# One core, three layers in one kernel: where low parts are made, in which order a mixture unit issues its steps, and when chunk loads go out

## The chip, the cores and the metric

The kernel runs on one core of one Trainium2 chip. The metric is the device time of one execution in microseconds; lower is better. The core's engines are TensorE (PE in the rows, PEld its weight loads), VectorE (DVE), ScalarE (ACT), GpSimd (POOL) and SyncE (SP), which issues most of the DMAs. Each engine works through its own queue in order.

## What is computed

The reference chains three layers. A Nyström attention over 4 batches, 8 heads and 576 positions gives a table of 2304 tokens by 512. Then a dense layer with a softplus in the middle, and then a layer of eight experts, of which each token uses one:

```python
h = x @ w_in                                        # 2304x512 by 512x2048
g = np.maximum(h, 0.0) + np.log1p(np.exp(-np.abs(h)))
x = g @ w_out                                       # 2304x2048 by 2048x512
logits = x @ w_gate;  e_idx = np.argmax(logits, 1)  # one of 8 experts per token
eom = 1 / (1 + np.exp(-(x @ w_output_gate)))
for e in range(8):
    h = np.maximum(x[mask] @ w1[e], 0.0)
    out[mask] = gate_w[mask, None] * eom[mask, e, None] * (h @ w2[e])
```

The weights of the dense layer arrive as 64-bit floats.

## The kernel before

**Products.** Every fp32 operand of the dense layer and the experts is kept as a high part (`hi`, an ACT copy to a shorter format) and a low part (`lo`, the rest: value minus high part, a subtraction on DVE or POOL). A product is three matmuls: hi by hi, hi by lo, lo by hi.

**The dense layer** (called mixture here) runs over nine chunks of 256 tokens and, in each, over eight pieces p of two 128-wide columns of `w_in`. One chunk and one piece make a unit, and the list `order` has 72 of them, i = 0 to 71. A unit issues: `gemm1`, 24 matmuls of 256 columns into `ps_h`; `softplus`, which makes `gh` and `gl`; and `gemm2`, 12 matmuls of 512 columns into the accumulators of its chunk, which is issued two units later (`LAG` = 2). So PE alternates between `gemm1(i)` and `gemm2(i-2)`. `ps_h` has two buffers, so `gemm1(i+2)` needs that `d` of unit i (the last pass that reads `ps_h`) is over.

**softplus** is four ACT passes (`t` by Abs, `t` by Exp, `u`, `l` by Ln), three DVE passes (`u`, `d`, `l`), the ACT pass `gh` (the high part of l) and the DVE pass `gl`. In the kernel before, all of it is issued in one go, ahead of `gemm2(i-2)`.

**Joint units.** The first 24 units (`nj` = 24, i = 0 to 23) go through chunks 0, 1 and 2 together, piece by piece, because the weights are still being decoded from 64-bit words then: piece p+1 of chunk 0, then piece p of chunks 1 and 2. The decode is 21 jobs, one for each 128-wide slice f of `w_in` (`whi`, `wlo`) or of `w_out` (`woh`, `wol`) that the attention stage has not prepared, in the order in which they are due. A job has three steps, taken with `units(n)`: `hi` (ACT, and the Abs of the next job, `deca`), `lo` (DVE), and the next job's three DVE passes (`dect`, `dect`, `deca`) with a load. `units(1)` stands at three places of softplus, so each unit from i = 1 does the work of one job; `EXTRA = 0, 5, 8` adds one more job in units 5 and 8.

**Chunks.** From unit 24 on, each chunk has eight units of its own. In its unit p = 5 it loads the next chunk (`load_xr`, SP) and splits it at once (`split_x`: `xh` on ACT, `xl` on DVE). Chunk 3 (`JOINT`) is loaded and split in unit 23. When `gemm2` has finished a chunk, its `gate` begins: two ACT copies of the accumulators (`x`, L679), transposes (`ps_tr` on PE, copied to `x2t` on ACT), logits (`ps_lg`), the choice of the expert and the rank (`sb`, `cd`, `oh`, `ps_rk`, `rmat`). `gate` is a generator in steps; one step is taken after `gemm1` (`next(side)`) and one after `gemm2`. In the units in which chunk 7 is gated (`fast`), further steps stand in the middle of `gemm1` and `gemm2` (`hook`). `early` follows the gate of chunk 7 (`ps_n`, `erhs`, `ps_i`) and finds the tokens of the first two expert slots.

**Expert slots.** A slot is 128 tokens of one expert. `splits` gives, eight steps a slot, the halves u = 0, 1 of four weight blocks i = 0 to 3: `hi` on ACT (L477), `lo` on DVE or POOL (L479). In slot 0 the four halves of blocks 2 and 3 and the second half of block 0 go to POOL. The gate of the last chunk and `route`, which assigns all other slots, run on DVE inside slots 0 and 1; the registers that choose the later weights come out of `route`.

The order of all queues from the mixture on is the program's own order (`manual_schedule`).

Of the kernel before, what the change touches and what calls it, by code (L numbers as in the profile page):

```python
# [12 lines left out]
F32R = DT.float32r  # L13
# [17 lines left out]
CH = 256  # L31
# [85 lines left out]
def moe_nystrom_kernel(ctx: ExitStack, tc: tile.TileContext, q, k, v, w_in, w_out, w_gate, w_ogate, w1, w2,  # L117
# [357 lines left out]
    def split(s, i, w, u):  # L475
        us = slice(2 * u, 2 * u + 2)
        nc.scalar.activation(w[0][:, us], raw[i][:, us], AF.Copy)  # L477
        eng = nc.gpsimd if s == 0 and i > 1 or i % 2 == 0 and u else nc.vector
        eng.tensor_tensor(w[1][:, us], raw[i][:, us], w[0][:, us].bitcast(F32), ALU.subtract)  # L479
# [65 lines left out]
    with ExitStack() as mctx:  # L545
# [94 lines left out]

        def softplus(h, units):

            t = sp.tile([128, 2, CH], F32, tag="t", name="t")
            u = sp.tile([128, 2, CH], F32, tag="u", name="u")
            l = sp.tile([128, 2, CH], F32, tag="l", name="l")
            d = sp.tile([128, 2, CH], F32, tag="d", name="d")
            gh = m3.tile([128, 2, CH], F32R, tag="gh", name="gh")
            gl = m3.tile([128, 2, CH], F32R, tag="gl", name="gl")
            nc.scalar.activation(t, h, AF.Abs)
            nc.scalar.activation(t, t, AF.Exp, scale=-1.0)  # L650
            nc.scalar.activation(u, t, AF.Identity, bias=1.0)  # L651
            nc.scalar.activation(l, t, AF.Ln, bias=1.0)
            units(1)
            nc.vector.scalar_tensor_tensor(u, u, -1.0, t, ALU.add, ALU.subtract)  # L654
            nc.vector.scalar_tensor_tensor(d, h, 0.0, u, ALU.max, ALU.subtract)  # L655
            nc.vector.tensor_tensor(l, l, d, ALU.add)  # L656
            nc.scalar.activation(gh, l, AF.Copy)  # L657
            units(1)
            nc.vector.tensor_tensor(gl, l, gh.bitcast(F32), ALU.subtract)  # L659
            units(1)  # L660
            return gh, gl

# [190 lines left out]
        with tc.manual_schedule():  # L853
# [28 lines left out]
            for i in range(len(order) + LAG):  # L882
# [11 lines left out]
                if i < len(order):  # L894
                    c, p = order[i]
                    if i == nj - 1:
                        xr.append(load_xr(JOINT))
                    h = gemm1(p, xs[c], *HB.get(i, ()))
                    if i > nj + LAG:
                        next(side, None)  # L900
                    gs[i] = softplus(h, units if i else int)
                    if i in EXTRA:
                        units(1 if i == 0 else 3)
                    if i == 2:
                        nc.vector.tensor_copy(tri_b, cc("tri"))
                        nc.vector.tensor_copy(one_b, cc("ones"))
                        nc.vector.memset(osum[:, 0], 0.0)
                        nc.vector.tensor_copy(sgn[:, 0], cc("iota")[:1, :NE])
                        nc.vector.tensor_scalar(sgn[:, 1], cc("iota")[:1, :NE], -1.0, None, ALU.mult)
                        for nm, src in ((0, w_gate), (1, w_ogate)):  # L910
                            nc.sync.dma_start(wg[:, :, nm * NE:(nm + 1) * NE], src.rearrange("(k p) e -> p k e", p=128))
# [178 lines left out]
```

## Time and profile before

| | |
|---|---|
| time, median of 3 runs | 910.09 us (909.3 to 910.9) |
| profiled execution | 910.2 us, of which the span from first to last instruction is 908.4 us |
| busy: PE, PEld | 859.9 us (95%), 718.9 us (79%) |
| busy: DVE, ACT, POOL | 666.5 us (73%), 586.9 us (65%), 209.5 us (23%) |
| mean granted TensorE clock | 0.988 of full speed |
| attention stage, joint units | to about 152 us; to 284 us |
| chunks 3 to 8 (units 24 to 71) | 284 to 600 us |
| expert slots | 600 to 908 us |

PE's busy share is modelled from its issue times, so what is read is its idle time: where PE waits, for whom, and how long the matmuls behind the wait take. A wait is put down to the releaser that came last. Times below are microseconds from the start of the span.

### The profile page before, as it was taken

Reading aid. Unit: us, or ns where it says so; the run is one execution under the profiler, and the core shown is the slowest. Engines: PE = TensorE matmul, PEld = TensorE weight load, DVE = VectorE, ACT = ScalarE, POOL = GpSimd, SP = SyncE. Lnnn points to the kernel's source line nnn. Section 1 sums busy time; section 2 is a strip of 40 time slices with the busy share of each in tenths; the row PEclk is TensorE's granted clock in tenths of the full one; section 3 lists DMA queues with packets and bytes.
Section 4 is the critical chain, followed back from the end, with each engine's and each line's share of the span. In section 5 each row is a group of like instructions: output and inputs, shape, how many; then the busy total and the mean of one; then the engine's idle time right before and its main releaser. Section 6 shows DMA issues by size and latency. Waiting matters only on the chain.

```text
span 908.4 us, 15419 instructions
## 1 busy us (share of the span) xinstructions
PE 859.9 (95%) x5826; PEld 718.9 (79%) x5826; DVE 666.5 (73%) x1121; ACT 586.9 (65%) x958; POOL 209.5 (23%) x109
## 2 busy tenths in 40 slices
PE   6998987989998999998999998989999999999996
PEld 3665655888997999998899997877888888888885
DVE  0856697999984465556556463668799999999994
ACT  2554565767774655555455554465888888888883
POOL 0001131000000000000000000034666667666662
PEclk9999999999999999999999999999999999999998
DMA  9856555333300000101011000141118369521600
GB/s 222 196 140 183 158 189 166 95 116 97 113 24 24 1 25 1 47 24 47 1 48 47 1 25 1 47 186 59 36 40 292 148 222 366 185 105 35 232 26 33
DMA packets 49516, 90.92 MB, mean 100 GB/s; under 512 B 5471, under 2 KB 32095, under 8 KB 47392
## 3 DMA queue, kind: packets, MB, share of 16 engines
q1 hardware_dynamic: 41408, 74.43, 26.6%
q0 software_dynamic: 3680, 10.78, 3.7%
q10 hardware_dynamic: 4352, 4.72, 1.5%
q8 instruction: 46, 0.75, 0.4%
q14 instruction: 30, 0.25, 0.1%
HBM read 134.46 MB, written 15.48 MB: 165 GB/s over the span
## 4 chain that ended last, share of the span: by engine, by line
PE 68%; DVE 14%; DMA 6%; ACT 6%; issue 4%; POOL 0%; SPq 0%; DVEq 0%; POOLq 0%; ACTq 0%
PE ps_h L635 19%; PE acc L670 15%; PE ps_g L960 10%; PE ps_y L985 9%; DMA raw<-in_moe_w 3%; DVE lo L479 2%; DVE dect L101 2%; PE ps_hT L974 2%; ACT hi L477 2%; PE ps_lg L695 2%; DVE deca L102 1%; PE ps_t L185 1%; PE ps_t L161 1%; DVE l L656 1%; DVE d L655 1%
## 5 line engine op out<-in xcount | busy, mean ns | idle before, releaser
L479 DVE TENSOR_TENSOR lo<-raw,hi 128x1024 fp32r<-128x1024 f32 x129 | 226.3, 1781 | 11.4 <-ACT hi L477 11.1
L477 ACT ACTIVATE hi<-raw 128x1024 fp32r<-128x1024 f32 x176 | 176.9, 1063 | 8.5 <-DMA raw<-in_moe_w 8.1
L635 PE MATMUL ps_h<-xh,whi 128*128 128x256 f32 x512 | 148.1, 289 | 7.7 <-DVE d L655 4.8
L635 PE MATMUL ps_h<-xl,whi 128*128 128x256 f32 x512 | 146.3, 286 | 0.4 <-DVE xl L108 0.4
L635 PE MATMUL ps_h<-xh,wlo 128*128 128x256 f32 x512 | 146.2, 286 | 0.0
L486 POOL DMA_INDIRECT xg<-x_d,gidx x23 | 37.0, 1610 | 444.1 <-ACT t L650 433.1
L479 POOL TENSOR_TENSOR lo<-raw,hi 128x1024 fp32r<-128x1024 f32 x47 | 116.7, 2485 | 35.8 <-ACT hi L477 35.6
L657 ACT ACTIVATE gh<-l 128x512 fp32r<-128x512 f32 x72 | 45.5, 632 | 116.0 <-DVE l L656 116.0
L654 DVE SCALAR_TENSOR_TENSOR u<-u,t 128x512 f32<-128x512 f32 x72 | 49.6, 688 | 83.5 <-ACT u L651 83.4
L635 PEld LDWEIGHTS ps_h<-xh,whi 128*128 128x128 f32 x512 | 99.2, 194 | 13.6 <-DVE d L655 6.1
L670 PE MATMUL acc<-woh,gh 128*128 128x512 f32 x256 | 103.1, 403 | 1.6 <-ACT gh L657 1.6
L670 PE MATMUL acc<-wol,gh 128*128 128x512 f32 x256 | 101.0, 394 | 0.0
L635 PEld LDWEIGHTS ps_h<-xl,whi 128*128 128x128 f32 x512 | 99.2, 194 | 2.2 <-DVE xl L108 0.6
L670 PE MATMUL acc<-woh,gl 128*128 128x512 f32 x256 | 100.8, 394 | 0.0
L635 PEld LDWEIGHTS ps_h<-xh,wlo 128*128 128x128 f32 x512 | 99.4, 194 | 0.0
L659 DVE TENSOR_TENSOR gl<-l,gh 128x512 fp32r<-128x512 f32 x72 | 49.9, 693 | 38.8 <-ACT gh L657 37.0
L985 PE MATMUL ps_y<-hi,woh 128*128 128x512 f32 x184 | 76.7, 417 | 0.2 <-ACT woh L977 0.2
L985 PE MATMUL ps_y<-hi,wol 128*128 128x512 f32 x184 | 73.3, 398 | 1.4 <-DVE wol L978 1.3
L960 PE MATMUL ps_g<-hi,x0l 128*128 128x512 f32 x184 | 73.9, 402 | 0.3
L985 PE MATMUL ps_y<-lo,woh 128*128 128x512 f32 x184 | 72.7, 395 | 0.0
L960 PE MATMUL ps_g<-hi,x0h 128*128 128x512 f32 x184 | 72.1, 392 | 0.0
L960 PE MATMUL ps_g<-lo,x0h 128*128 128x512 f32 x184 | 71.9, 391 | 0.0
(246 smaller groups left out, 1756.6 us busy)
## 6 DMA issues: line engine op xcount, KB each, us to landing
raw<-in_moe_w SPq DMA_DIRECT2D x88, 1024.0 KB
raw<-in_moe_w_in SPq DMA_DIRECT2D x16, 512.0 KB
raw<-in_moe_w_out SPq DMA_DIRECT2D x16, 512.0 KB
x_d<-x SPq DMA_DIRECT2D x9, 514.0 KB
k<-in_k SPq DMA_DIRECT2D x8, 576.0 KB
q<-in_q SPq DMA_DIRECT2D x8, 576.0 KB
v<-in_v SPq DMA_DIRECT2D x8, 576.0 KB
xT_d<-xo ACTq DMA_DIRECT2D x16, 288.0 KB
```

The source lines that it names most:

```text
L101: nc.vector.scalar_tensor_tensor(t, hi32, -0x80000000, t, ALU.bitwise_and, ALU.bitwise_or)
L477: nc.scalar.activation(w[0][:, us], raw[i][:, us], AF.Copy)
L479: eng.tensor_tensor(w[1][:, us], raw[i][:, us], w[0][:, us].bitcast(F32), ALU.subtract)
L486: nc.gpsimd.indirect_dma_start(out=xg, out_offset=None, in_=src, in_offset=bass.IndirectOffsetOnAxis(ap=gidx[:, s:s + 1], axis=0))
L635: nc.tensor.matmul(ps[:, i], a[:, kk], b_[:, kk], start=n == 0, stop=n == 11)
L654: nc.vector.scalar_tensor_tensor(u, u, -1.0, t, ALU.add, ALU.subtract)
L657: nc.scalar.activation(gh, l, AF.Copy)
L659: nc.vector.tensor_tensor(gl, l, gh.bitcast(F32), ALU.subtract)
L670: nc.tensor.matmul(acc[tt], a[:, i, ts_], b_[f], start=f == 0 and n == 0, stop=f == NFF - 1 and n == 2)
L695: nc.tensor.matmul(pl[:, :2 * NE], xt[tt][:, kk], wg[:, kk], start=kk == 0, stop=kk == 3)
L960: nc.tensor.matmul(ps, a[:, kk], b_[:, kk], start=n == 0, stop=n == 11)
L985: nc.tensor.matmul(y, a[:, kk], b_[:, kk], start=half == 0 and n == 0, stop=half == 1 and n == 11)
```

## The change

Six edits. `EXTRA` becomes three further steps in unit 15 instead of those in units 5 and 8. The weight steps are taken only in joint units. `softplus` becomes a generator in four parts: `gemm1(i)`, the gate step behind it and the four ACT passes come first, then the three DVE passes, then `gemm2(i-2)`, the first ACT copies of a gate, and the gate step behind `gemm2`, and only then `gh`, a weight step, `gl`. `load_xr` moves from p = 5 to the end of p = 3 (chunk 3: unit 21), `split_x` stays at p = 5 (chunk 3: unit 22 instead of 23). And all eight low parts of slot 0 go to DVE.

```diff
-EXTRA = 0, 5, 8
+EXTRA = 15, 15, 15
...
-        eng = nc.gpsimd if s == 0 and i > 1 or i % 2 == 0 and u else nc.vector
+        eng = nc.gpsimd if s and i % 2 == 0 and u else nc.vector
...
             nc.scalar.activation(l, t, AF.Ln, bias=1.0)
-            units(1)
+            yield
             nc.vector.scalar_tensor_tensor(u, u, -1.0, t, ALU.add, ALU.subtract)
             nc.vector.scalar_tensor_tensor(d, h, 0.0, u, ALU.max, ALU.subtract)
             nc.vector.tensor_tensor(l, l, d, ALU.add)
+            yield
+            gh = m3.tile([128, 2, CH], F32R, tag="gh", name="gh")
+            gl = m3.tile([128, 2, CH], F32R, tag="gl", name="gl")
             nc.scalar.activation(gh, l, AF.Copy)
-            units(1)
+            yield
             nc.vector.tensor_tensor(gl, l, gh.bitcast(F32), ALU.subtract)
-            units(1)
-            return gh, gl
+            yield gh, gl
...
                     c, p = order[i]
-                    if i == nj - 1:
-                        xr.append(load_xr(JOINT))
-                    h = gemm1(p, xs[c], *HB.get(i, ()))
+                    g = softplus(gemm1(p, xs[c], *HB.get(i, ())))
                     if i > nj + LAG:
                         next(side, None)
-                    gs[i] = softplus(h, units if i else int)
-                    if i in EXTRA:
-                        units(1 if i == 0 else 3)
...
-                    if i == nj - 1:
-                        xs[JOINT] = split_x(xr.pop(0))
-                    if p == 5 and JOINT - 1 < c < NCH - 1:
-                        xs[c + 1] = split_x(load_xr(c + 1))
+                    next(g)
+                    if 0 < i < nj:
+                        units(1)
+                    next(g)
...
                 if nj + LAG < i < len(order) + LAG - 1:
                     next(side, None)
+                if i < len(order):
+                    next(g)
+                    if 0 < i < nj:
+                        units(1)
+                    gs[i] = next(g)
+                    if i < nj:
+                        units(1 + EXTRA.count(i))
...
+                    if i == nj - 3 or p == 3 and JOINT - 1 < c < NCH - 1:
+                        xr.append(load_xr(max(c + 1, JOINT)))
+                    if i == nj - 2 or p == 5 and JOINT - 1 < c < NCH - 1:
+                        xs[max(c + 1, JOINT)] = split_x(xr.pop(0))
```

PE's queue holds the same instructions in the same order in both kernels. Three places of the other queues follow.

DVE in unit 15 and the beginning of the next. The rows of one job are `wlo` or `wol` (its low part; 2002 is the tile of slices 8 to 15 of `w_in`) and `dect`, `dect`, `deca` (the decode of the next one). Before:

```order
L654 SCALAR_TENSOR_TENSOR u<-u,t 128x512
L655 SCALAR_TENSOR_TENSOR d<-ps_h,u 128x512
L656 TENSOR_TENSOR l<-l,d 128x512
L599 TENSOR_TENSOR wol_2071<-deca,woh_2058 128x512
L659 TENSOR_TENSOR gl<-l,gh 128x512
L100 TENSOR_SCALAR dect<-deca 128x512
L101 SCALAR_TENSOR_TENSOR dect<-raw,dect 128x512
L102 SCALAR_TENSOR_TENSOR deca<-raw,dect 128x512
```

Now:

```order
L652 SCALAR_TENSOR_TENSOR u<-u,t 128x512
L653 SCALAR_TENSOR_TENSOR d<-ps_h,u 128x512
L654 TENSOR_TENSOR l<-l,d 128x512
L599 TENSOR_TENSOR wlo_2002<-deca,whi_2001 128x4x128
L660 TENSOR_TENSOR gl<-l,gh 128x512
L100 TENSOR_SCALAR dect<-deca 128x512
L101 SCALAR_TENSOR_TENSOR dect<-raw,dect 128x512
L102 SCALAR_TENSOR_TENSOR deca<-raw,dect 128x512
L599 TENSOR_TENSOR wol_2070<-deca,woh_2057 128x512
L100 TENSOR_SCALAR dect<-deca 128x512
L101 SCALAR_TENSOR_TENSOR dect<-raw,dect 128x512
L102 SCALAR_TENSOR_TENSOR deca<-raw,dect 128x512
```

The decode stands two jobs further back than before: unit 15 now makes the low part of slice 13 of `w_in` (before, unit 13 did), and unit 18 that of slice 15. Slice 13 is read by `gemm1` of unit 16, in its second half, and slice 15 by that of unit 19; on PE these matmuls carry a wait for DVE.

ACT in units 65 and 66, where the gate of chunk 7 begins (6256 and 6252 are the same tile in the two kernels). Before:

```order
L652 ACTIVATE l<-t 128x512
L657 ACTIVATE gh<-l 128x512
L679 ACTIVATE x_6256<-acc_5816 128x512
L679 ACTIVATE x_6256<-acc_5817 128x512
L690 ACTIVATE x2t<-ps_tr 128x512
L649 ACTIVATE t<-ps_h 128x512
L650 ACTIVATE t<-t 128x512
L651 ACTIVATE u<-t 128x512
L652 ACTIVATE l<-t 128x512
L657 ACTIVATE gh<-l 128x512
L690 ACTIVATE x2t<-ps_tr 128x512
```

Now:

```order
L650 ACTIVATE l<-t 128x512
L679 ACTIVATE x_6252<-acc_5812 128x512
L679 ACTIVATE x_6252<-acc_5813 128x512
L658 ACTIVATE gh<-l 128x512
L690 ACTIVATE x2t<-ps_tr 128x512
L647 ACTIVATE t<-ps_h 128x512
L648 ACTIVATE t<-t 128x512
L649 ACTIVATE u<-t 128x512
L650 ACTIVATE l<-t 128x512
L690 ACTIVATE x2t<-ps_tr 128x512
L658 ACTIVATE gh<-l 128x512
```

The accumulator copies and the second `x2t` have changed places with `gh`.

DVE in slot 0, from the rank of the last chunk to `rmat`. Before:

```order
L732 TENSOR_TENSOR z<-lg,oh 128x16
L733 TENSOR_REDUCE s_6882<-z 128x2
L736 TENSOR_TENSOR cd<-ps_rk,oh 128x16
L737 TENSOR_REDUCE rk<-cd 128x2
L740 TENSOR_TENSOR q__6890<-rk,cst 128x34
L742 TENSOR_REDUCE rd<-q__6890 128x2
L743 SCALAR_TENSOR_TENSOR rk<-rd,rk 128x2
L978 TENSOR_TENSOR wol_79<-ps_hT,woh_76 128x512
L978 TENSOR_TENSOR wol_80<-ps_hT,woh_77 128x512
L746 TENSOR_SCALAR rmat<-cst,rk 128x128 x2
```

Now:

```order
L479 TENSOR_TENSOR lo_6803<-raw_6701,hi_6802 128x1024 x2
L732 TENSOR_TENSOR z<-lg,oh 128x16
L733 TENSOR_REDUCE s_6882<-z 128x2
L736 TENSOR_TENSOR cd<-ps_rk,oh 128x16
L737 TENSOR_REDUCE rk<-cd 128x2
L740 TENSOR_TENSOR q__6890<-rk,cst 128x34
L742 TENSOR_REDUCE rd<-q__6890 128x2
L743 SCALAR_TENSOR_TENSOR rk<-rd,rk 128x2
L984 TENSOR_TENSOR wol_79<-ps_hT,woh_76 128x512
L479 TENSOR_TENSOR lo_6801<-raw_6702,hi_6800 128x1024 x2
L984 TENSOR_TENSOR wol_80<-ps_hT,woh_77 128x512
L746 TENSOR_SCALAR rmat<-cst,rk 128x128 x2
```

Four low parts (blocks 2 and 3) now stand between the choice of the expert and `rmat`; the fifth, of block 0, stands further ahead, behind the first half of the same block. On POOL only the gathers are left there.

## Rows read from the trace of the kernel before

**Rows 1.** Page, costliest groups: operation, shapes, count; busy, mean ns; idle before
```profile
L657 ACT ACTIVATE gh<-l 128x512 fp32r<-128x512 f32 x72 | 45.5, 632 | 116.0 <-DVE l L656 116.0
```

**Rows 2.** PE, joint units: total waits (us, times, longest), then timeline rows (start, us, operation)
```profile
PE ps_h L635 <- DVE d L655: 4.8, 3, 2.4
...
177.34 0.39 PE L635 MATMUL ps_h<-xh,whi 128*128 128x256 f32 x1 [0.24 <-DVE d L655]
...
278.11 0.28 PE L635 MATMUL ps_h<-xh,whi 128*128 128x256 f32 x1
```

**Rows 3.** DVE timeline, units 4 to 6: start, us, line, operation
```profile
175.81 0.68 DVE L654 SCALAR_TENSOR_TENSOR u<-u,t 128x512 f32<-128x512 f32 x1
178.00 0.68 DVE L599 TENSOR_TENSOR wol<-deca,woh 128x512 fp32r<-128x512 f32 x1
181.18 0.69 DVE L654 SCALAR_TENSOR_TENSOR u<-u,t 128x512 f32<-128x512 f32 x1
...
189.74 0.68 DVE L654 SCALAR_TENSOR_TENSOR u<-u,t 128x512 f32<-128x512 f32 x1
```

**Rows 4.** PE timeline: first matmuls of the products of units 24 and 25
```profile
286.73 0.38 PE L635 MATMUL ps_h<-xh,whi 128*128 128x256 f32 x1 [2.83 <-ACT xh L107]
...
294.65 0.28 PE L635 MATMUL ps_h<-xh,whi 128*128 128x256 f32 x1
```

**Rows 5.** Timelines of ACT and PE in chunk 5, behind unit p = 5
```profile
428.32 1.15 ACT L107 ACTIVATE xh<-xr 128x512 fp32r<-128x512 f32 x2 [1.60 <-DMA xr<-xT_d]
430.01 1.07 PE L695 MATMUL ps_lg<-wg,x2t 128*128 128x16 f32 x8 [2.51 <-ACT x2t L690]
```

**Rows 6.** Chain that ended last: start, us, whole first (L635) and second (L670) products
```profile
210.57 3.14 PE ps_h L635 x24
...
431.07 4.31 PE acc L670 x12
...
442.48 2.87 PE ps_h L635 x24
445.36 2.75 PE acc L670 x12
...
561.67 4.47 PE ps_h L635 x24
```

**Rows 7.** PE's waits from 440 to 600: us in total, times, longest
```profile
PE ps_n L767 <- DVE cd L736: 1.8, 1, 1.8
PE ps_tr L689 <- ACT x L679: 1.8, 2, 1.4
PE ps_lg L695 <- ACT x2t L690: 1.4, 1, 1.4
```

**Rows 8.** Timelines: DVE and POOL in slot 0, two DVE rows from chunk 7, PE's wait
```profile
573.11 0.48 DVE L746 TENSOR_SCALAR rmat<-cst,rk 128x128 bf16<-128x128 f32 x2
574.43 0.23 DVE L771 SCALAR_TENSOR_TENSOR cd<-ps_n,mx,cst 128x8 f32<-128x8 f32 x1
...
598.03 1.23 DVE L479 TENSOR_TENSOR lo<-raw,hi 128x1024 fp32r<-128x1024 f32 x1 [0.30 <-issue]
606.30 4.70 POOL L479 TENSOR_TENSOR lo<-raw,hi 128x1024 fp32r<-128x1024 f32 x2 [4.78 <-ACT hi L477]
606.79 1.94 DVE L717 TENSOR_TENSOR sb<-lg,mx 128x16 f32<-128x16 f32 x1
608.76 2.27 DVE L718 SCALAR_TENSOR_TENSOR cd<-sb,cst 128x16 f32<-128x16 f32 x1
611.50 0.17 PE L726 MATMUL ps_rk<-oh,tri_b 128*128 128x16 bf16 x1 [2.34 <-DVE oh L720]
614.10 4.74 POOL L479 TENSOR_TENSOR lo<-raw,hi 128x1024 fp32r<-128x1024 f32 x2 [3.10 <-ACT hi L477]
615.49 0.69 DVE L978 TENSOR_TENSOR wol<-ps_hT,woh 128x512 fp32r<-128x512 f32 x1 [1.69 <-ACT woh L977]
616.10 2.82 DVE L746 TENSOR_SCALAR rmat<-cst,rk 128x128 bf16<-128x128 f32 x2
```

More of the change, by code (lines that the diff above doesn't have):

```diff
@@ L639, in gemm1, with softplus @@
             return ps
-        def softplus(h, units):
+        def softplus(h):
             t = sp.tile([128, 2, CH], F32, tag="t", name="t")
@@ L646, in softplus @@
             d = sp.tile([128, 2, CH], F32, tag="d", name="d")
-            gh = m3.tile([128, 2, CH], F32R, tag="gh", name="gh")
-            gl = m3.tile([128, 2, CH], F32R, tag="gl", name="gl")
             nc.scalar.activation(t, h, AF.Abs)
@@ L895, in moe_nystrom_kernel @@
                     c, p = order[i]
-                    if i == nj - 1:
-                        xr.append(load_xr(JOINT))
-                    h = gemm1(p, xs[c], *HB.get(i, ()))
+                    g = softplus(gemm1(p, xs[c], *HB.get(i, ())))
                     if i > nj + LAG:
                         next(side, None)
-                    gs[i] = softplus(h, units if i else int)
-                    if i in EXTRA:
-                        units(1 if i == 0 else 3)
[L904 to L911, printed above, removed]
-                    if i == nj - 1:
-                        xs[JOINT] = split_x(xr.pop(0))
-                    if p == 5 and JOINT - 1 < c < NCH - 1:
-                        xs[c + 1] = split_x(load_xr(c + 1))
+                    next(g)
+                    if 0 < i < nj:
+                        units(1)
+                    next(g)
                 if i >= len(order):
@@ L932, in moe_nystrom_kernel @@
                     next(side, None)
+                if i < len(order):
[5 more added lines that the diff above has]
+                        units(1 + EXTRA.count(i))
+                    if i == 2:
+                        nc.vector.tensor_copy(tri_b, cc("tri"))
+                        nc.vector.tensor_copy(one_b, cc("ones"))
+                        nc.vector.memset(osum[:, 0], 0.0)
+                        nc.vector.tensor_copy(sgn[:, 0], cc("iota")[:1, :NE])
+                        nc.vector.tensor_scalar(sgn[:, 1], cc("iota")[:1, :NE], -1.0, None, ALU.mult)
+                        for nm, src in ((0, w_gate), (1, w_ogate)):
+                            nc.sync.dma_start(wg[:, :, nm * NE:(nm + 1) * NE], src.rearrange("(k p) e -> p k e", p=128))
+                    if i == nj - 3 or p == 3 and JOINT - 1 < c < NCH - 1:
+                        xr.append(load_xr(max(c + 1, JOINT)))
+                    if i == nj - 2 or p == 5 and JOINT - 1 < c < NCH - 1:
+                        xs[max(c + 1, JOINT)] = split_x(xr.pop(0))
             side = chain(side, route())
```

## The prediction

> **What bounds the kernel now.** TensorE's order of work does not change, and it is busy nearly throughout, so I look only for the places where it waits, in the order of the program: first its own waits by releaser, then its timeline at each, then the queue of the engine that it waits for, and last whether the matmuls behind the wait run slower. There are five such places that the change touches.
>
> In the joint units TensorE waits for `d` of VectorE three times, 4.8 us in all, at most 2.4 [rows 2]. From 177.34 to 278.11 it does 17 units [rows 2]; at 2.87 + 2.75 = 5.62 us each [rows 6] that is 95.5 of 100.8 us, so 5.2 us are lost. VectorE needs 5.37 us a unit (175.81 to 181.18), but 8.56 us in unit 5 (181.18 to 189.74), where a second job stands [rows 3]: 3.19 us more. It starts with a lag, works that off at 5.62 - 5.37 = 0.25 us a unit, and each added job brings the lag back.
>
> At the end of the joint units the first product of chunk 3 waits 2.83 us for `xh` [rows 4], which is split behind `gh` and `gl` of unit 23. Between the starts of units 23 and 25 lie 294.65 - 278.11 = 16.54 us [rows 2, 4] instead of 11.24: 5.3 us lost, matmuls at the lower clock included.
>
> In chunk 5, ACT holds the split of the next chunk 1.60 us for its DMA, the transposed gate tile stands behind it, and TensorE waits 2.51 us for that [rows 5]. The second product behind it takes 4.31 instead of 2.75 us [rows 6]: together 4.1 us lost.
>
> Between 440 and 600 TensorE waits 1.8 us for accumulator copies, 1.4 us for an `x2t` and 1.8 us for a `cd` [rows 7]; one first product behind these takes 4.47 instead of 2.87 us [rows 6]. All three releasers stand behind `gh` or `gl` in their queues, and ACT idles 116 us in front of `gh` over the 72 units, 1.6 us in each [rows 1]: a hole in which these copies fit.
>
> In slot 0 TensorE waits 2.34 us for `oh`, and around it three small VectorE passes take 1.94, 2.27 and 2.82 us while POOL is in a low part; the same kinds take 0.23 and 0.48 us in chunk 7 [rows 8].
>
> **The change part by part.** The sum is made against the profiled execution, 910.2 us (0.1 above the median of the three runs).
>
> *Extra steps at 15.* Removed: two added jobs of 3.19 us on VectorE, and with them the 5.2 us that TensorE lost. Moved: the one job at 15, and the whole decode two jobs back from unit 5 on. With no extra job, `u` of unit n starts at 181.18 + 5.37(n - 5) and `gemm1(n)` at 177.34 + 5.62(n - 6) [rows 2, 3, 6]. Up to unit 15 that is free of waits. But the low part of slice 13 is now made in unit 15 and read in unit 16. It starts 2.19 us after `u` (175.81 to 178.00) and takes 0.68 [rows 3]: 234.88 + 2.87 = 237.75. `gemm1(16)` starts at 233.54, and reads it as the third matmul of its second half, 14 of 24 matmuls or 1.67 us in: 235.2. New wait: 2.5 us. The high part, one ACT pass earlier, takes the first 0.5 or so of this. In unit 18 the same happens to slice 15: `u` starts at 181.18 + 13 x 5.37 + 3.19 = 254.18, the low part ends at 257.05, `gemm1(19)` starts at 177.34 + 13 x 5.62 + 2.5 = 252.9 and needs it at 254.6. New wait: 2.45 us. The job added at 15 would hold `gemm1(18)` by 0.1 us, which the first of these waits hides. So 5.2 us go and 5.0 come: **0.2 us saved**. Bounds: 5.2 if VectorE were so far ahead that slices 13 and 15 are in time; -3.0 if the clock falls at both new waits (below).
>
> *Split of chunk 3 one unit earlier.* `xh` and `xl` now stand behind unit 22. `gh` of unit 23 ended at about 286.1, one copy of 0.6 before 286.73 [rows 4]; that of unit 22 ends a unit earlier, at 280.5, and `gemm1(24)` can start at 278.11 + 5.62 = 283.7. Into these 3.2 us go the pair of copies, 1.15 [rows 5], and the second subtraction, 0.69 (a pass of the size of `u`, [rows 3]): 1.9. The load goes out one unit further ahead still. What is late next is `d` of unit 22 for the `ps_h` buffer, which is over before the split begins. **5.3 us saved**; bound below: 3, if the split is late by the rest.
>
> *Chunk loads at p = 3.* Two units are 11 us; the DMA wait of 1.60 us goes. At the other four loads no wait of TensorE hangs on it. SyncE's queue: the load moves past at most one store of a finished gate, and waits for nothing else, since its buffers were released a chunk ago.
>
> *Gate steps inside the unit.* The five waits named above lose their releaser: `x2t` in chunk 5 stands ahead of the split and of `gh`, so the **4.1 us** go. The accumulator copies run as soon as `gemm2` ends, in the hole: **1.8 us**. The `x2t` of chunk 7 also stands ahead of `gh`: **1.4 us**, and with the two waits before it the slow product: 4.47 - 2.87 = **1.6 us**. The `cd` comes ahead of `gh` and `gl`, that is 0.63 [rows 1] + 0.69 (`gl`, again of the size of `u`) earlier, so 0.5 of 1.8 stays; but `gl` now stands behind the rank and ahead of `early`, and can hold `ps_i` by up to its 0.69. I take **0.7 us**; the bounds are 0.6 and 1.3. What is added: `gh` and `gl` stand behind the second product of the unit before last. `gh` then ends at about 2.87 + 2.75 + two copies of 1.1 together + 0.63 = 7.3 us after the start of its unit; `gemm2` reads it at 2 x 5.62 + 2.87 = 14.1. And `l`, which has one buffer, is free before the next Ln. So nobody waits, and that costs nothing.
>
> *Low parts of slot 0.* Removed from POOL: five halves. Returned to VectorE: 1.74 of `sb` (taking 0.2 for a pass of this kind), 2.04 of `cd`, 2.34 of `rmat`, in all 6.1 us [rows 8]. Added in the chain from `oh` to `route`: four halves of 1.23 us, 4.9 us; of these up to 1.69 lie in a wait that was there before `wol` [rows 8]. 6.1 - 4.9 + 1.7 = 2.9; I take off 0.3 for waits on the two `hi` passes: **2.6 us saved**, since loads and gathers of all later slots hang on `route`. Bounds: 0 and 2.9. The fifth half lies ahead of the chain, where VectorE is early for the logits; I put it at nothing, and at 1.23 if it is not early.
>
> The Trainium skill has advice against this edit: "Perfetto Trace Analysis", section "Optimizing Scalar/DVE Operations", says that work may well leave a saturated VectorE, even for GpSimd, but adds that the two share a port. "SBUF — State Buffer", section "Who interferes with whom", says that a VectorE pass with two SBUF inputs and a GpSimd pass that reads SBUF exclude each other for a whole instruction. By that rule the trace agrees: `sb` ends at 608.7, halfway through POOL's pair that runs from 606.30 to 611.00 [rows 8]. By the advice alone the edit would cost time; that is a rival below.
>
> The sum: 0.2 + 5.3 + 4.1 + 1.8 + 1.4 + 1.6 + 0.7 + 2.6 = 17.7 us. 910.2 - 17.7 = **892.5 us**. From 660 us on nothing is changed but the start.
>
> **The rivals.**
>
> *The clock falls behind the new waits.* After the waits of 2.83 and 2.51 us products took 1.6 us longer, after one of 2.17 (210.57) the product took 3.14, no slow one [rows 2, 4, 6]. The two new waits, 2.5 and 2.45, lie between, with two matmuls inside each; a third of about 1.4 us remains in slot 0. One such case costs 1.6: 894.1; all three 4.8: 897.3.
>
> *The weights are in time.* If VectorE were faster in units 6 to 15 than 5.37 us, slices 13 and 15 would not be waited for: 892.5 - 5.0 = 887.5. Against it: unit 4 has the same passes as units 6 to 14 now have, and takes 5.37 [rows 3].
>
> *The small passes are not slow because of POOL.* Then 6.1 us do not come back, and the four halves lengthen the chain by 4.9 - 1.7 = 3.2: 892.5 + 2.6 + 3.2 = 898.3. For it: VectorE is the busier engine. Against it: the coincidence in time, three out of three.
>
> *Slower: `gh` waits for TensorE, and TensorE for `gh`.* Behind `gemm2(i-2)` now stand the copies or a gate step, then `gh`, `gl`, then the next unit. If these steps took more than 14.1 - 7.3 = 6.8 us, or if the rank step held `gl` until the next Ln, each gate would hold TensorE by a second product, 2.75 us. With nine gates that is 25 us: 892.5 + 25 = 917. Against it: the passes of these steps take 0.2 to 0.5 us each [rows 8], and none has ten of the long ones.
>
> *The change does not do what it says*: the waits return with other releasers of the same length, 910.
>
> **How the numbers follow.** Forecast 0.57; clock 0.20; weights in time 0.08; small passes 0.07; slower 0.04; no change 0.02; 0.02 for anything else. The range reaches from the weights-in-time case, with half a microsecond of its own error inside, to that of the small passes: **888 to 898.5**; it takes in the clock cases. What one can tell from no change here is about 0.2%, 1.8 us. Faster: 0.57 + 0.20 + 0.08 + 0.07 + 0.02 = 0.94; same 0.02; slower 0.04.
>
> **What would show it right or wrong.** In the timeline of the changed kernel TensorE should have no wait for `d` of more than 0.3 us after 177, two waits of about 2.5 us for `wlo` (each led by a short one for `whi`) some 56 and 76 us after it, no wait for `xh` at the beginning of chunk 3, none for `x2t` or accumulator copies, and short ones, each under 0.8 us, for `ps_n` and `ps_i`. Slot 0 should show `sb`, `cd` and `rmat` at 0.2 to 0.5 us, an empty POOL until the gathers, and `route` done about 2.6 us earlier after the last product of the mixture. It would be wrong if the `wlo` waits are missing, if their products are slow, or if waits for `gh` or `gl` appear at second products.

## The result, and the profile after

The changed kernel takes 894.77 us (median of four runs, 892.69 to 897.02), beside 909.69 us for the kernel before on the same chip: a ratio of 0.9836, 95% interval 0.9802 to 0.9869. Two more sets of the same changed kernel, below, gave 893.20 and 894.21 us. The forecast of 892.5 was 2.3 us low, and its range of 888.0 to 898.5 holds the time. The profiled execution took 892.98 us, its span 891.2 against 908.4: 17.2 us less, where the sum had 17.7.

TensorE's waits from 176.9 to 616 us, that is from unit 6 on into the expert slots (us in total, times, longest), which answer to [rows 2, 4, 5, 7]:

```profile
PE ps_h L635 <- DVE wlo L599: 3.3, 2, 1.6
PE ps_y L991 <- DVE wol L984: 2.0, 1, 2.0
PE ps_h L635 <- ACT whi L596: 0.8, 2, 0.5
PE ps_y L991 <- ACT woh L983: 0.7, 1, 0.7
PE ps_i L791 <- DVE erhs L786: 0.5, 1, 0.5
PE ps_n L767 <- DVE cd L736: 0.4, 1, 0.4
PE ps_h L635 <- DVE d L653: 0.2, 1, 0.2
...
```

The waits for `xh`, `x2t` and `oh` are gone, those for `d`, `x` and `cd` nearly. What is new is `wlo`, twice, led by `whi`. PE's timeline shows where (start, us, operation, wait):

```profile
176.78 0.39 PE L635 MATMUL ps_h<-xh,whi 128*128 128x256 f32 x1 [0.23 <-DVE d L653]
...
235.18 0.39 PE L635 MATMUL ps_h<-x0h,whi 128*128 128x256 f32 x1 [0.53 <-ACT whi L596]
...
237.32 0.39 PE L635 MATMUL ps_h<-x0h,wlo 128*128 128x256 f32 x1 [1.64 <-DVE wlo L599]
...
254.49 0.38 PE L635 MATMUL ps_h<-x0h,whi 128*128 128x256 f32 x1 [0.29 <-ACT whi L596]
...
256.63 0.58 PE L635 MATMUL ps_h<-x0h,wlo 128*128 128x256 f32 x1 [1.63 <-DVE wlo L599]
...
278.96 0.28 PE L635 MATMUL ps_h<-xh,whi 128*128 128x256 f32 x1
...
290.20 0.28 PE L635 MATMUL ps_h<-xh,whi 128*128 128x256 f32 x1
```

From unit 6 to unit 23 it is 278.96 - 176.78 = 102.2 us, 1.4 more than before [rows 2]; from unit 23 to unit 25 it is 11.24 instead of 16.54, 5.3 less. The matmul at 256.63 takes 0.58, that at 237.32 only 0.39: behind the second wait the clock fell. The stretches behind the first wait and behind the second (us, then busy time of each engine, PEclk, DMA share, GB/s):

```profile
237.40:243.00 5.60, 5.60 (x36) 5.11 (x37) 4.77 (x9) 3.06 (x6) 0.00 (x0) 1.00 0.30 99
256.70:260.00 3.30, 3.30 (x13) 3.09 (x14) 2.38 (x4) 0.74 (x2) 0.00 (x0) 0.53 0.00 0
```

From 256.70 to 260.00 the granted clock is 0.53, the 1.2 GHz level for nearly all of it; against matmuls at the usual 0.12 us spacing that stretch lost 1.5 us.

Slot 0, timelines of DVE, PE and POOL, the answer to [rows 8]:

```profile
591.84 0.17 DVE L717 TENSOR_TENSOR sb<-lg,mx 128x16 f32<-128x16 f32 x1
...
592.94 2.36 DVE L479 TENSOR_TENSOR lo<-raw,hi 128x1024 fp32r<-128x1024 f32 x2
...
597.29 2.36 DVE L479 TENSOR_TENSOR lo<-raw,hi 128x1024 fp32r<-128x1024 f32 x2 [0.17 <-ACT hi L477]
...
600.17 0.47 DVE L746 TENSOR_SCALAR rmat<-cst,rk 128x128 bf16<-128x128 f32 x2
...
608.35 0.94 POOL L486 DMA_INDIRECT xg<-x_d,gidx  x1 [39.40 <-DVE wol L984]
...
615.71 0.50 PE L991 MATMUL ps_y<-hi,wol 128*128 128x512 f32 x1 [1.99 <-DVE wol L984]
```

The small passes (`sb`, `cd` behind it, `rmat`) fell from 1.94, 2.27 and 2.82 to 0.17, 0.17 and 0.47 us, POOL is empty up to the gathers, and the wait for `wol` at the end of the stretch grew from 1.33 to 1.99 us.

To see where the time went, the span is cut at places that both PE queues have: S up to `gemm1(6)`; A to the first `ps_tr` of a gate (joint units, split of chunk 3); B to `ps_n` (the chunks); C to the first `ps_i`; then 17.35 us that are the same everywhere; D from the first matmul of slot 0 to the second `ps_i`, in `route`; E the rest. The rows below "changed" are the experiments.

| profiled execution | S | A | B | C | D | E | span |
|---|---|---|---|---|---|---|---|
| before | 177.34 | 134.18 | 260.75 | 4.37 | 29.26 | 285.15 | 908.4 |
| changed | 176.78 | 130.28 | 249.57 | 4.97 | 26.23 | 286.02 | 891.2 |
| changed, second set | 176.99 | 130.36 | 249.57 | 4.96 | 26.19 | 285.98 | 891.4 |
| changed, third set | 177.37 | 130.40 | 249.56 | 4.97 | 26.31 | 286.13 | 892.1 |
| added job at 14 | 177.51 | 131.46 | 249.57 | 4.96 | 26.44 | 287.70 | 895.0 |
| added jobs at 5, 8 | 178.44 | 130.27 | 249.56 | 4.97 | 26.17 | 288.23 | 895.0 |
| steps at 12, 13, 14 | 177.68 | 132.80 | 249.56 | 4.96 | 26.27 | 287.97 | 896.6 |
| low part first | 177.62 | 129.54 | 249.55 | 4.97 | 26.39 | 287.87 | 893.3 |
| `gh` ahead again | 177.58 | 130.45 | 257.49 | 4.37 | 26.33 | 285.82 | 899.4 |
| loads at p = 5 again | 177.91 | 128.88 | 253.24 | 4.97 | 26.16 | 287.89 | 896.4 |
| split at 23 again | 178.59 | 135.22 | 249.56 | 4.97 | 26.19 | 287.71 | 899.6 |
| low parts on POOL again | 178.12 | 128.86 | 249.57 | 4.97 | 29.45 | 285.27 | 893.6 |
| POOL busy for nothing | 179.57 | 128.88 | 249.55 | 4.97 | 33.70 | 284.78 | 898.8 |

Changed against before: S -0.6, A -3.9, B -11.2, C +0.6, D -3.0, E +0.9, together -17.2 us.

### The profile page after: what moved, and what is told of

Its sections match the earlier page's. It is cut to its first block, busy times and chain, and to the rows that moved or that the text cites. A ratio compares the mean times of both kernels' runs of the same rounds, so it can differ in the third digit from the quotient of the medians.

```text
span 891.2 us, 15413 instructions
## 1 busy us (share of the span) xinstructions
PE 854.5 (96%) x5826; PEld 715.9 (80%) x5826; DVE 665.3 (75%) x1126; ACT 587.4 (66%) x958; POOL 200.9 (23%) x104
## 5 line engine op out<-in xcount | busy, mean ns | idle before, releaser
L479 DVE TENSOR_TENSOR lo<-raw,hi 128x1024 fp32r<-128x1024 f32 x134 | 233.1, 1767 | 10.4 <-ACT hi L477 9.9
L477 ACT ACTIVATE hi<-raw 128x1024 fp32r<-128x1024 f32 x176 | 176.9, 1063 | 9.8 <-DMA raw<-in_moe_w 8.6
L635 PE MATMUL ps_h<-xh,whi 128*128 128x256 f32 x512 | 147.1, 287 | 0.2 <-DVE d L653 0.2
L635 PE MATMUL ps_h<-xl,whi 128*128 128x256 f32 x512 | 145.2, 284 | 0.0
L635 PE MATMUL ps_h<-xh,wlo 128*128 128x256 f32 x512 | 145.2, 284 | 0.0
L486 POOL DMA_INDIRECT xg<-x_d,gidx x23 | 38.8, 1685 | 461.2 <-ACT t L648 418.2
L479 POOL TENSOR_TENSOR lo<-raw,hi 128x1024 fp32r<-128x1024 f32 x42 | 106.2, 2528 | 12.2 <-ACT hi L477 9.9
L658 ACT ACTIVATE gh<-l 128x512 fp32r<-128x512 f32 x72 | 45.4, 631 | 90.7 <-DVE l L654 90.7
L670 PE MATMUL acc<-woh,gh 128*128 128x512 f32 x256 | 102.6, 401 | 0.6 <-ACT gh L658 0.6
L635 PEld LDWEIGHTS ps_h<-xh,whi 128*128 128x128 f32 x512 | 98.4, 192 | 3.6 <-ACT t L647 0.8
L670 PE MATMUL acc<-wol,gh 128*128 128x512 f32 x256 | 100.6, 393 | 0.0
L670 PE MATMUL acc<-woh,gl 128*128 128x512 f32 x256 | 100.1, 391 | 0.0
L635 PEld LDWEIGHTS ps_h<-xl,whi 128*128 128x128 f32 x512 | 98.5, 192 | 1.7
L635 PEld LDWEIGHTS ps_h<-xh,wlo 128*128 128x128 f32 x512 | 98.4, 192 | 0.0
```

The source lines that it names most:

```text
L486: nc.gpsimd.indirect_dma_start(out=xg, out_offset=None, in_=src, in_offset=bass.IndirectOffsetOnAxis(ap=gidx[:, s:s + 1], axis=0))
L635: nc.tensor.matmul(ps[:, i], a[:, kk], b_[:, kk], start=n == 0, stop=n == 11)
L670: nc.tensor.matmul(acc[tt], a[:, i, ts_], b_[f], start=f == 0 and n == 0, stop=f == NFF - 1 and n == 2)
```

## The experiments

Each is the changed kernel with one thing altered; diffs are against it.

### The same kernel again

> The changed kernel once more, unaltered, on another chip run, because its four executions fell into two groups, 892.7 and 893.0 against 896.6 and 897.0. Theory: the 4 us between them are TensorE's clock, which falls behind the late-weight wait of unit 19 in one group (the profile shows a product 1.4 us too long there) and at one or two places more in the other. Then the two groups come again, and a profile of the slower group shows one or two slow products more and the same waits. Rival: the two chips differ from the beginning; then all executions here lie in one group, and the waits are the same.

893.20 us (892.1 to 895.03), ratio 0.9813 (0.9789 to 0.9837). The two groups of the first four executions did not come again: four of these five lie from 892.1 to 893.5, one at 895.0. The waits are those of the first profile within 0.02 us for `wlo`, and the clock falls behind unit 19 again (A 130.36).

> The changed kernel once more, beside the two others on the same chip, as their reference: 893 to 895 us. Slow matmuls of about 1.5 us behind the wait at unit 19, or about 618 us, may or may not show in this execution; the waits themselves should be those of the first profile to 0.1 us (2.17 at unit 16, 1.92 at unit 19, none for xh, x2t or accumulator copies).

894.21 us (892.75 to 896.33), ratio 0.9822 (0.98 to 0.9843); waits 0.51 + 1.63 and 0.31 + 1.63. A to E of the three profiles agree within 0.15 us. All three are profiles of executions that took 893 to 894 us; none of those that took 896 to 897 was profiled, so what makes those longer is not shown. What differs between all the profiles here, where the edits are the same, is S and the clock at certain places (below). S differs mostly in the attention stage, which the change does not touch: the mixture's first product starts at 136.41 us before and at 135.79 now.

### Where the added job stands

```diff
-EXTRA = 15, 15, 15
+EXTRA = 14, 14, 14
```

> One number changed: the added decode job stands in unit 14 instead of 15, so that slices 13 and 15 are made one unit earlier than they are read. Late-weight theory: both pairs of waits in units 16 and 19 (0.53 + 1.64 and 0.29 + 1.63 in the changed kernel's trace) go, and the 1.4 us of slow matmuls behind the second; in exchange the first product of unit 17 waits about 0.4 us for d. 4.1 + 1.4 - 0.4 = 5 us less than the changed kernel: 888 for its faster executions. Rival (VectorE is the bound there, and a wait that goes at one unit comes at the next): within 1 us of the changed kernel, with waits for d in units 16 to 20.

894.76 us, ratio 0.982 (0.9788 to 0.9851): no gain. PE's timeline at units 16 and 19:

```profile
235.90 0.39 PE L635 MATMUL ps_h<-x0h,whi 128*128 128x256 f32 x1 [0.49 <-ACT whi L596]
...
255.20 0.39 PE L635 MATMUL ps_h<-x0h,whi 128*128 128x256 f32 x1 [1.70 <-ACT whi L596]
...
257.33 0.58 PE L635 MATMUL ps_h<-x0h,wlo 128*128 128x256 f32 x1 [1.63 <-DVE wlo L599]
```

The wait at unit 16 fell to 0.71 us (0.49 and one of 0.22 behind it), and that at unit 19 rose to 3.33: 4.04 together, 4.09 in the changed kernel. The low part of slice 15 is still made in unit 18, behind the same VectorE work, and TensorE cannot pass it; what it does not wait for at 16, it waits for at 19. (A is 1.2 us longer only because the matmuls behind unit 19 were slow for longer, with 2.7 us lost.)

```diff
-EXTRA = 15, 15, 15
+EXTRA = 5, 5, 5, 8, 8, 8
```

> The changed kernel with the added decode jobs back in units 5 and 8, all else as changed. The sum of the prediction has 5.2 us lost by these two jobs against 5.0 by the late weights: 0.2 us slower than the changed kernel without its slow matmuls, so 1.2 us faster than its faster executions, 891.8, with two waits for d of 2.4 and 2.2 us and none for wlo. If moving the jobs was worth more than that, it is slower than the changed kernel by what they are worth.

894.85 us, ratio 0.9826 (0.98 to 0.9852). PE waits for `d` as before, 2.43 and 2.18 us, and not for `wlo`. A is 130.27, that of the changed kernel (both hold a slow stretch of 1.5 us, here behind the second of these waits): moving the jobs from 5 and 8 to 15 is worth nothing. The time expected, 891.8, was 3 us too low; in the profiled execution, the longest of the four (896.78), this stretch, S (1.7 us more than in the first profile of the changed kernel) and E (2.2 more) make up the difference.

```diff
-EXTRA = 15, 15, 15
+EXTRA = 12, 13, 14
```

> The added job spread: one of its three steps in each of units 12, 13 and 14. VectorE does the same work, 2.47 us, without the 0.7 us in which it waits for the high part in one unit; by unit 14 it has 0.24 + 9 x 0.25 = 2.5 us in hand. Late-weight theory: no wait at all from unit 7 to 23, 5.5 us less than the changed kernel's faster executions, 887.5. Rival: as in the run with unit 14, no gain.

898.38 us, ratio 0.9858 (0.9829 to 0.9887): slower than the changed kernel, A by 2.5 us. The joint units' waits (us in total, times, longest):

```profile
PE ps_h L635 <- DVE d L653: 2.3, 3, 1.4
PE ps_h L635 <- DVE wlo L599: 1.9, 2, 1.6
PE ps_h L635 <- ACT whi L596: 1.9, 2, 1.7
```

Both kinds of wait are there, for `d` and for the weights. With single steps added, what a unit takes at each of its places shifts by a step or two from unit 12 on, and VectorE itself now waits for ScalarE in units 12, 13 and 14, 3.1 us where the changed kernel has one such wait, of 0.70:

```profile
225.30 0.69 DVE L599 TENSOR_TENSOR wol<-deca,woh 128x512 fp32r<-128x512 f32 x1 [0.70 <-ACT woh L596]
...
227.69 0.69 DVE L652 SCALAR_TENSOR_TENSOR u<-u,t 128x512 f32<-128x512 f32 x1 [1.70 <-ACT u L649]
...
237.83 0.69 DVE L660 TENSOR_TENSOR gl<-l,gh 128x512 fp32r<-128x512 f32 x1 [0.70 <-ACT gh L658]
```

Slice 15's low part starts 81.5 us after the end of S, 79.1 in the changed kernel: the 2.4 us between them are the loss in A.

```diff
             nc.vector.scalar_tensor_tensor(u, u, -1.0, t, ALU.add, ALU.subtract)
+            yield
             nc.vector.scalar_tensor_tensor(d, h, 0.0, u, ALU.max, ALU.subtract)
...
+LO1 = 15, 18
...
                     next(g)
+                    if i in LO1:
+                        units(1)
+                    next(g)
...
-                    if 0 < i < nj:
+                    if 0 < i < nj and i not in LO1:
                         units(1)
```

> The changed kernel, but in units 15 and 18 the low part of the weight slice stands between u and d on VectorE, not behind l; nothing else moves. It is then made 1.4 us earlier (two passes of 0.69), in both units. Theory (the two waits for wlo at units 16 and 19 together are set by all that VectorE does ahead of the low part of slice 15): the wait at unit 16 falls from 2.17 to about 0.8 us; the one at unit 19 stays at about 1.9, because it comes earlier by what was saved at 16; together 2.7 instead of 4.1 us, so 1.4 us less, and without the slow matmuls behind unit 19 up to 2.9 less: 890.5 to 893.5 where the changed kernel takes 893.2 to 894.8. Rival (d and l of these units, each 0.69 us later, are then waited for): new waits for d or for gl of 0.3 us or more at units 17 to 20, the same time or slower.

892.88 us (891.48 to 895.08), ratio 0.9797 (0.9777 to 0.9817); the changed kernel on the same chip 894.21. PE's waits and DVE's rows, in unit 18 and (the last) in unit 15:

```profile
236.03 0.38 PE L636 MATMUL ps_h<-x0h,whi 128*128 128x256 f32 x1 [0.53 <-ACT whi L597]
...
236.76 0.39 PE L636 MATMUL ps_h<-x0h,wlo 128*128 128x256 f32 x1 [0.22 <-DVE wlo L600]
...
255.86 0.39 PE L636 MATMUL ps_h<-x0h,whi 128*128 128x256 f32 x1 [1.78 <-ACT whi L597]
...
256.59 0.39 PE L636 MATMUL ps_h<-x0h,wlo 128*128 128x256 f32 x1 [0.22 <-DVE wlo L600]
```

```profile
255.06 0.69 DVE L653 SCALAR_TENSOR_TENSOR u<-u,t 128x512 f32<-128x512 f32 x1
255.84 0.69 DVE L600 TENSOR_TENSOR wlo<-deca,whi 128x512 fp32r<-128x512 f32 x1
...
238.73 0.69 DVE L662 TENSOR_TENSOR gl<-l,gh 128x512 fp32r<-128x512 f32 x1 [0.70 <-ACT gh L660]
```

0.75 + 2.00 = 2.75 us, where 2.7 was expected, and no wait for `d` or `gl` came instead; new is one of 0.18 for `wlo` in the first half of `gemm1(19)`. But slice 15's low part is made only 0.9 us earlier (78.2 us after the end of S instead of 79.1), not 1.4, because VectorE itself now waits 0.70 us for `gh` in unit 15. That VectorE's time up to slice 15's low part, its own waits included, sets the sum of TensorE's waits is shown from three sides: moving the job leaves it (4.04), taking two passes out from ahead of that low part cuts it to 2.93, and 2.4 us more of waiting on VectorE raise it (5.9, with the steps at 12, 13 and 14). The gain in time, 1.3 us between the medians and 0.8 in A, is in line, but the intervals of the two ratios overlap; it is the fastest kernel here by a hair, and not shown to be faster.

### The order of the gate steps, and the loads

The block from `gemm2` to the gate step behind it is put behind `gh`, the weight steps and `gl` again, as before (shown as the moved lines):

```diff
                     next(g)
-                if i >= LAG:
...
-                    gemm2(p2, gs.pop(i - LAG), accs[c2])
...
-                if nj + LAG < i < len(order) + LAG - 1:
-                    next(side, None)
                 if i < len(order):
...
                         xs[max(c + 1, JOINT)] = split_x(xr.pop(0))
+                if i >= LAG:
...
+                    gemm2(p2, gs.pop(i - LAG), accs[c2])
...
+                if nj + LAG < i < len(order) + LAG - 1:
+                    next(side, None)
```

> The changed kernel, but gh, gl, the chunk loads and the splits stand ahead of the second product and the gate step again, as they did; loads still at p = 3, split of chunk 3 in unit 22, extra steps at 15, low parts of slot 0 on VectorE. Order theory: the waits for accumulator copies (1.8), for x2t (1.4), for cd (1.8 instead of 0.9 for cd and erhs) and the slow product of 1.6 come back; in chunk 5 x2t stands behind gh and a split that no longer waits for its DMA, so TensorE waits about 1 us there. 6 to 7 us slower than the changed kernel. Rival (the gain between 290 and 577 came from the earlier loads): within 1 us of the changed kernel.

901.01 us, ratio 0.989 (0.9868 to 0.9913). B rises by 7.9 us, and the waits of the kernel before are back in the chunks (compare [rows 7]):

```profile
PE ps_lg L695 <- ACT x2t L690: 2.2, 2, 1.4
PE ps_tr L689 <- ACT x L679: 2.0, 3, 1.4
PE ps_n L767 <- DVE cd L736: 1.8, 1, 1.8
```

In chunk 5 only 0.8 of the 2.51 us [rows 5] returns, and no slow product: there the earlier load alone does most of it.

```diff
-                    if i == nj - 3 or p == 3 and JOINT - 1 < c < NCH - 1:
+                    if i == nj - 3 or p == 5 and JOINT - 1 < c < NCH - 1:
```

> The changed kernel with the loads of chunks 4 to 8 back at p = 5, in front of their splits; chunk 3 as changed. Theory: the split waits for its DMA again, about 1.6 us on ScalarE, but x2t now stands ahead of it, and the next unit's first ACT pass has 2 us in hand, so TensorE loses nothing: the same as the changed kernel within 1 us. Rival (the early load is what ended the wait of 2.5 us in chunk 5): about 4 us slower, with that wait back.

898.29 us, ratio 0.9862 (0.984 to 0.9883): not the same within 1 us, B is 3.7 us longer. In chunk 5 there is no wait; the loss lies in the chunks behind it. SyncE's queue and ACT's at the first place:

```profile
473.05 0.36 SPq L751 DMA_DIRECT2D x_d<-x  x1
473.51 1.35 SPq L615 DMA_DIRECT2D xr<-xT_d  x2
```

```profile
477.25 1.38 ACT L107 ACTIVATE xh<-xr 128x512 fp32r<-128x512 f32 x2 [4.68 <-DMA xr<-xT_d]
```

With the gate steps inside the unit, the gate's last store (`x_d`) is issued ahead of the load, so the load goes out only when the gate is finished, and ACT holds the split for 4.68 us. `d` of the next unit is late behind that, and so is `gemm1` two units on: PE waits 1.5 us for `d`, in two places, 1.0 for `x` and 0.4 for an `x2t`. From B of four kernels: before 260.75, loads moved alone (`gh` ahead again) 257.49 (-3.3), steps moved alone (loads at p = 5 again) 253.24 (-7.5), both 249.57 (-11.2). The two edits add up, to within 0.4 us.

### The split of chunk 3

```diff
-                    if i == nj - 2 or p == 5 and JOINT - 1 < c < NCH - 1:
+                    if i == nj - 1 or p == 5 and JOINT - 1 < c < NCH - 1:
```

> The changed kernel with one thing put back: chunk 3 is split in unit 23, as before, instead of 22; its load stays two units ahead and gh, gl and the gate steps stay where the change has them. Theory (the split was late because it stood behind the gate's high and low part of the unit before the first product that needs it): the two ACT copies now stand behind gh of unit 23 again, TensorE waits about 2.8 us for xh at the first product of chunk 3, a slow product of about 1.6 us more may follow, and the time is 4 to 5.3 us above the changed kernel (about 898). Rival (what was late in the kernel before was the load, issued in the same unit as the split; with the load two units ahead the split itself is in time): no wait for xh, the same time within 1 us (894 to 895).

900.89 us (896.8 to 902.02), ratio 0.9879 (0.9856 to 0.9901), where about 898 was expected; A is 4.8 us above the third set's. PE at the first product of chunk 3, and ACT ahead of it:

```profile
287.95 0.58 PE L635 MATMUL ps_h<-xh,whi 128*128 128x256 f32 x1 [2.83 <-ACT xh L107]
```

```profile
286.75 0.63 ACT L658 ACTIVATE gh<-l 128x512 fp32r<-128x512 f32 x1 [1.83 <-DVE l L654]
287.28 1.13 ACT L107 ACTIVATE xh<-xr 128x512 fp32r<-128x512 f32 x2
```

The same wait as before to the hundredth, although the load goes out two units ahead: it was the place behind `gh`, not the load. From unit 23 to unit 25 it is 17.60 us (279.34 to 296.94) instead of 11.24: 6.4 us lost, more than the 5.3 of the kernel before, because the clock stays low for longer (0.53 on average from 287.90 to 295.00). A shows only 4.8 of it, since the joint units were 1.5 shorter in this execution: the clock fell behind unit 16, not behind unit 19.

### The low parts of slot 0

```diff
-        eng = nc.gpsimd if s and i % 2 == 0 and u else nc.vector
+        eng = nc.gpsimd if s == 0 and i > 1 or i % 2 == 0 and u else nc.vector
```

> Only the edit of slot 0 is undone: five of the eight low parts of slot 0 go back to GpSimd. Port theory: sb, cd and rmat take about 1.9, 2.3 and 2.8 us again, TensorE waits about 2.3 us for oh, and the kernel is 2.2 to 2.6 us slower than the changed one. Rival (the long passes have another cause, and the added low parts lengthen the chain): the small passes were slow or short regardless, and the kernel is up to 3 us faster than the changed one.

895.02 us, ratio 0.9823 (0.98 to 0.9845). The small passes are slow again, and TensorE waits for `oh`:

```profile
591.62 1.95 DVE L717 TENSOR_TENSOR sb<-lg,mx 128x16 f32<-128x16 f32 x1
...
601.15 2.83 DVE L746 TENSOR_SCALAR rmat<-cst,rk 128x128 bf16<-128x128 f32 x2
```

```profile
596.34 0.17 PE L726 MATMUL ps_rk<-oh,tri_b 128*128 128x16 bf16 x1 [2.32 <-DVE oh L720]
```

D rises by 3.2 us, and E falls by 0.75: behind a later `route` the wait for `wol` is shorter (1.61). In the time itself the 2.2 to 2.6 us expected do not show (895.02, and medians of 893.2 to 894.8 for the changed kernel); that the edit saves about 2.5 us is read from D and E.

The next one leaves VectorE all eight low parts and lets POOL make four of them a second time, into a buffer that is not in use then:

```diff
         eng = nc.gpsimd if s and i % 2 == 0 and u else nc.vector
+        if s == 0 and i > 1:
+            nc.gpsimd.tensor_tensor(ring[0][0][1][:, us], raw[i][:, us], w[0][:, us].bitcast(F32), ALU.subtract)
```

> The changed kernel, in which GpSimd makes the low parts of blocks 2 and 3 of slot 0 a second time, into a tile that nobody reads; VectorE's work and all waits between engines stay as changed. It does work that is not needed. Port theory: while GpSimd is in one of these four passes (2.35 us each), VectorE passes with two inputs in SBUF stand still, so sb and cd take about 2 us each again, low parts up to 3.5 us, and the kernel is 4 to 7 us slower than the changed one. Rival (VectorE's passes are slow for another reason): VectorE's passes take 0.2 and 1.23 us as in the changed kernel, and the time is the same within 0.5 us.

899.83 us, ratio 0.9878 (0.9856 to 0.99); D rises by 7.5 us: TensorE waits 2.32 us for `oh`, 1.69 for `woh` and 2.03 at the second `ps_i`, and the clock falls behind the second of these.

```profile
593.26 1.96 DVE L719 TENSOR_TENSOR sb<-lg,mx 128x16 f32<-128x16 f32 x1
...
602.60 4.54 DVE L481 TENSOR_TENSOR lo<-raw,hi 128x1024 fp32r<-128x1024 f32 x2 [0.17 <-ACT hi L477]
```

```profile
592.78 4.71 POOL L480 TENSOR_TENSOR lo<-raw,hi 128x1024 fp32r<-128x1024 f32 x2 [22.46 <-ACT hi L477]
602.70 6.71 POOL L480 TENSOR_TENSOR lo<-raw,hi 128x1024 fp32r<-128x1024 f32 x2 [5.21 <-issue]
```

VectorE does the same work as in the changed kernel, and its 0.17 us passes take 1.96 (`sb`) and 2.27 (`cd`) as soon as POOL subtracts beside them; where both subtract long tiles, each is longer (4.54 for 2.36, 6.71 for 4.71). So POOL's passes make VectorE's slow, not the amount of VectorE's own work. That is what "SBUF — State Buffer", section "Who interferes with whom", of the Trainium skill says of such pairs, and the two rows of `sb` (0.17 and 1.96) agree.

## Why the prediction held, and where it was off

**Joint units: forecast 0.2 saved, 1.4 lost.** The waits for `d` went and those for `wlo` came, as worked out: 2.17 us at unit 16 (forecast 2.5) and 1.92 at unit 19 (2.45). What made the difference is the clock behind unit 19, 1.5 us. In the four experiments in which it fell behind unit 16 instead (loads at p = 5, split at 23, low parts on POOL, POOL busy), the stretch from unit 6 to unit 23 takes 100.75 to 100.77 us, as before (100.77 [rows 2]): without the fall at 19 the edit is worth 0.0. The rival "the clock falls behind the new waits" came true at one of its three places, at the price given (1.6). All three profiles of the changed kernel show it there, and slow products behind these waits are one of the prediction's own signs of being wrong; so what failed is the choice between the two cases (0.57 against 0.20), not the mechanism. That rival's time, 894.1, is also nearer to two of the three medians than 892.5 is.

**A price of mine was wrong in kind.** I priced each such fall alike. Where it comes behind unit 16, the wait at unit 19 takes it back: in the kernel with the low parts on POOL the clock fell behind unit 16, the wait at 19 shrank to 0.75, and A is 128.86, less than the 130.3 of the changed kernel. TensorE has to be at slice 15 when VectorE is, no sooner, so what it loses ahead of that is free.

**Split of chunk 3: forecast 5.3, measured 5.30**; put back, the 2.83 us wait returns, and 6.4 us with it.

**The chunks: forecast 9.6, measured 11.18 - 0.60 = 10.6.** The two PE queues, laid side by side from the first `ps_tr` (311.52 and 307.06), drift apart at these places: chunk 5 by 4.36 us (forecast 4.1), accumulator copies 0.55 + 0.14 + 1.59 = 2.28 (1.8), `x2t` of chunk 7 1.57 (1.4), the slow product 1.59 (1.6), `cd` and `erhs` 1.38 - 0.60 = 0.78 (0.7). For example the logits of chunk 5 start at 430.01 and 422.88: 118.49 and 115.82 us after that mark, 2.67 apart for a wait of 2.51. A wait's row is some 0.2 short of what its removal brings, and four of them (2.51, 0.38, 1.37 and 1.36 us) are most of the missing microsecond.

**The loads: right sum, wrong reason.** I wrote that of the loads only chunk 5's touched TensorE. That held in the old order. In the new one a load left at p = 5 would stand behind the gate's store and cost 3.7 us: I had looked at what the load moves past, not at what the moved gate steps put in front of it. And chunk 5's 4.1 us I booked on the gate steps alone; either edit removes most of it.

**Slot 0: forecast 2.6, measured 2.2, and by another path**: 3.0 in D less 0.9 in E. I added up VectorE's passes up to `route`, because later loads and gathers hang on it. But TensorE waits in neither kernel at the second `ps_i`, in `route`, and behind 640 us it has no wait of 0.3 us or more in either. Laid side by side, the PE queues drift apart by 2.57 us at the wait for `oh`, come 0.58 closer at that for `woh` (0.21 before, 0.72 now), drift 1.0 apart in the stretch behind it, where the clock was low before and is not now, and come 0.77 closer at the longer wait for `wol`. The two stretches, before and changed:

```profile
613.60:616.20 2.60, 2.60 (x7) 1.97 (x7) 0.91 (x3) 1.86 (x3) 2.10 (x1) 0.50 0.00 0
```

```profile
596.30:598.80 2.50, 2.36 (x9) 1.66 (x10) 2.29 (x5) 2.40 (x4) 0.00 (x0) 1.00 0.00 0
```

The clock and the two longer waits were in no term of the sum; together they come to only -0.35, and that the size came out so near is in part luck. The term that I took off for waits on `hi`, 0.3, was 0.17.

**The start**, S, gave 0.6 us that no edit explains; over twelve profiles it lies between 176.8 and 179.6. The parts are off by -1.6 (joint units), +1.0 (chunks), -0.4 (slot 0) and +0.6 (start) us: that the whole comes within 0.5 us of the sum in the profiled execution is in part that these cancel.

**The rivals.** Weights in time: out, both waits are there. Small passes not slow because of POOL: out, by the idle POOL and by the duplicates. `gh` waiting for TensorE in a ring: out, no second product waits for `gh` in the chunks; ACT's idle time in front of `gh` is now 90.7 us instead of 116.0 [rows 1], which fits the copies having gone into that hole. Of the experiments' expectations three failed outright: that one added job at 14 would save 5 us, that the place of the chunk loads would not matter, and that spreading the steps would save 5.5 us. Four more were off in a part: the two groups of executions, the times of the kernels with the jobs at 5 and 8 and with the split at 23, and what the low parts on POOL cost in time.

## What to carry to other kernels

Add up the producer's work, and its own waits, ahead of the last thing that the consumer needs: if that sets the sum of the waits, moving work about ahead of it only moves the wait, and what helps is to move work behind it. A step that only feeds something two units ahead should not stand in front of a step that somebody waits for now. And when steps are moved, read each queue from both ends: what they now pass, and what they now stand in front of.

## What the runs showed of the hardware

**The same wait does not always cost the same.** Behind unit 16's wait for `wlo`, 1.63 or 1.64 us long each time, the clock stayed at 1.00 in the changed kernel (237.40 to 243.00, above) and fell in the one with the low parts on POOL (and in three others):

```profile
238.70:241.70 3.00, 3.00 (x12) 2.90 (x13) 2.42 (x4) 0.47 (x1) 0.00 (x0) 0.50 0.05 18
```

Behind the wait for `wol` in slot 0 it is the other way about: after 2.42 us, in the third set of the changed kernel, it stayed; after 2.19, in the kernel with the low part first, it fell:

```profile
616.60:619.20 2.60, 2.60 (x12) 2.14 (x13) 2.60 (x3) 0.58 (x2) 2.44 (x2) 1.00 0.27 101
```

```profile
616.50:619.20 2.70, 2.70 (x8) 2.03 (x7) 2.70 (x3) 0.31 (x1) 2.68 (x2) 0.50 0.26 97
```

E follows: 285.8 to 286.1 us in the four profiles in which all eight low parts are VectorE's alone and the clock stayed there, 287.7 to 288.2 in the six in which it fell. So the length of the wait does not decide it, and no run here shows what does. Together with S this is as large as the scatter of one kernel's runs, 892.7 to 897.0; that it is its cause was not tested run by run.

**POOL and VectorE lengthen each other's subtractions** when both run long tiles: 4.54 and 6.71 us, where VectorE's pair takes 2.36 with POOL idle and POOL's takes 4.71 beside VectorE's small passes.
